# Windowed attention and a gated feed-forward block on one core: two heads in one double PSUM bank, feed-forward tiles of two blocks

## The chip, the cores and the metric

The kernel runs on one core of a Trainium2 chip. The metric is the device time of one execution in microseconds. The engines are TensorE (PE, matmuls), VectorE (DVE), ScalarE (ACT), GpSimd (POOL) and SyncE (SP, which issues most transfers). The tables of one core show all.

## The reference

Eight batches with eight heads each have 512 local and 32 global tokens of dimension 64. Local tokens see the global ones and the local ones within 32 positions; global tokens see all. The result, 4608 tokens of 512 features, goes through a feed-forward block with 2048 hidden units.

```python
s_ll = np.where(np.abs(pos[:, None] - pos[None, :]) <= 32, scale * q_l @ k_l.T, -1e9)
a_l = sm(np.concatenate([scale * q_l @ k_g.T, s_ll], axis=-1))
out_l = a_l @ np.concatenate([v_g, v_l])
out_g = sm(scale * q_g @ k_all.T) @ v_all
x = np.concatenate([out_g, out_l]).transpose(0, 2, 1, 3).reshape(4608, 512)
h = x @ w_in
sp = np.maximum(h, 0.0) + np.log1p(np.exp(-np.abs(h)))
out = (h * erf(sp)) @ w_out
```

## The kernel before

**The work.** Each float32 factor of the feed-forward block is split in two fp32r parts (names ending in h and l: xh, xl, winh, winl, wouth, woutl, gh, gl), and each product is three matmuls. The 4608 tokens are nine chunks: chunks 0 to 7 hold the 512 local tokens of a batch, chunk 8 the 256 global ones. The hidden units come in two halves, ps = 0 and ps = 1. For each chunk and half, `unit` (L1154) makes h for 256-row blocks in a PSUM bank and copies it to an SBUF tile hs; `gate` (L1180) runs softplus and erf on ScalarE (sp), multiplies by hs, rounds to gh and takes the rest gl; `project` (L1225) adds gh and gl times w_out into one PSUM bank per 128 tokens (op), which is evicted to os and stored. Half 0 leaves its sum in DRAM (part), half 1 adds it.

For half 1 of chunks 0 to 6, h is made by a scheme of seven products in place of eight: `seven_x` (L1055) forms sums of blocks of x (tx), `sums` (L1011) sums of weights (s0 to s3), and `quad` (L1103) runs seven products of 6 matmuls with 256 columns into four banks, two products in a bank, and adds them up on VectorE into two hs tiles. It does so for one column block of 128 hidden units at a time. Two of the four banks come from the pool ps_h (2 banks), two from ps_a (6 banks), which also serves attention and op.

The local attention (`attention`, L440) goes by windows of 32 rows on TensorE: scores of two heads into two banks s, a mask by matmul for the first heads (PREMASK of them) or on VectorE after that, maximum, exponential on ScalarE (sm). For the first TURN heads TensorE transposes the probabilities by matmul with the unit matrix ci; for the later ones VectorE does it in blocks of 32 (tp) and DMAs put the blocks in place (px, pt). `weighted` (L561) multiplies them by v (va, vb) into a bank o for each head, `weighted_end` (L589) divides by the sums into xn. `attention_global` (L694) does the global tokens of four heads in banks ga, gb and go, with GTURN in the role of TURN.

**The order.** All of these are entered with `Program.add` (L109) as operations with a planned duration per engine, a key and the tiles that they read and write. `Program.schedule` (L146) plays the engines through and emits the instructions in the order it finds: the ready operation with the least key, if its pool has a free tile. The numbers at the top of the file (HKEYS, QLEAD, WIN, LATE, AHEAD, SLACK and so on) set keys and limits. Where TensorE would idle before 53.6 us of the plan, it emits fillers, bf16 matmuls without use named spare. Waits between engines are semaphores that are put in for each tile. All engine calls go through helpers, so the profile's lines are those of the helpers: L348 (matmul), L349 (transpose), L350 (ScalarE), L351 (table load), L355 (DMA), L369 (VectorE and GpSimd). Names of tiles tell the place.

Of the kernel before, what the change touches and what calls it, by code (L numbers as in the profile page):

```python
# [20 lines left out]
P = 128  # L21
# [7 lines left out]
HKEYS = ((0, -7.804), (4, -5.172), (22, 1.403), (26, 7.192), (64, 43.381))  # L29
STEP, GKEY = 0.022, (-0.257, 0.006, -0.123)  # L30
QLEAD, VLEAD, RLEAD, XLEAD = (1.228, 0.782), (0.938, 0.499), 0.376, (1.072, 1.028, 1.005)
GOFF, POFF = (1.522, 1.5, 1.286), (4.244, 4.773, 2.878)
WIN, WOUT = (-5.905, -7.31, 0.441, -0.227), (10.721, 6.881, 8.147, 4.216)
LATE = (60.36, 53.234, 57.783, 66.337, 69.212, 67.928, 72.773, 74.4)
BIAS, AHEAD = 0.851, 10.286
# [12 lines left out]
BORROW = {"sm": ("sp", 7), "pt": ("hs", 7), "xn": ("gh", 5), "xT": ("gl", 5)}  # L48
# [3 lines left out]
BLOCK, ENTRY, FETCH = 256, 196, (5.06, 2.915)  # L52
START, RUSH, FETCHED = 2.5, 33.0, 1.0088
SWITCH, TRADE, CHOICE = 0.095, 0.092, 1

NBIAS, PREMASK = 5, 25
MLEAD = -5.339
# [3 lines left out]
PLAIN, MERGE = 0, 0  # L61
SEVEN = (0, 1, 2, 3, 4, 5, 6)
SUMS = (81.404, 83.062)

TURN, GTURN = 22, 6
GSPLIT = 4
# [18 lines left out]
class Buf:  # L85


    def __init__(self, pool, shape, dtype, name, tag, bufs=1):
        self.pool, self.shape, self.dtype, self.name, self.tag, self.bufs = pool, shape, dtype, name, tag, bufs
        self.users, self.ap = 0, None  # L90
        self.view = None
        self.writers, self.readers = [], []
# [6 lines left out]
class Program:  # L99
# [46 lines left out]
    def schedule(self):  # L146
# [74 lines left out]
        while events or any(o.eng is None for o in self.ops) and ahead < 1e3:  # L221
# [14 lines left out]
            while picked:  # L236
                picked = False
                for e, q in ready.items():
# [3 lines left out]
                    while until[e] <= now:  # L242
                        found = []
                        while q and len(found) < (CHOICE if e == "PE" else 1) and q[0][0] <= line[front].key + ahead:
# [4 lines left out]
                            need = {}  # L249
                            for b in op.new:  # L250
                                need[b.pool, b.tag] = need.get((b.pool, b.tag), 0) + 1
                            if any(free[k] < n for k, n in need.items()) or elsewhere(op, e):
# [42 lines left out]
                        for o in op.outs:  # L295
                            o.waits -= 1
                            o.at = max(o.at, t + (o.slack if e not in o.ways else 0.0))
# [12 lines left out]
def kernel(  # L310
# [29 lines left out]
    ps_a = ctx.enter_context(tc.tile_pool(name="ps_a", bufs=6, space=bass.MemoryType.PSUM))  # L340
# [53 lines left out]
    M16 = Buf(mp, [P, 512], F32, "mask16", "os", 2)  # L394
# [25 lines left out]
    def abuf(shape, name, tag, bufs):  # L420
# [4 lines left out]
        kind, n, h = name.split("_")[:3]  # L425
        if name == "vb_0_2":
# [3 lines left out]
        if kind in BORROW and int(n) * H + int(h) < FIRST:  # L430
            tag, bufs = BORROW[kind]
            b = Buf(mp, [P, SL], F32, name, tag, bufs)
            b.view = [P, 4, P]
# [3 lines left out]
    def psum_a(shape, name):  # L437
# [987 lines left out]
```

## Time and profile before

| | |
|---|---|
| median of 3 runs | 905.34 us (904.95 to 906.1) |
| profiled execution | 909.01 us, span 907.2 us |
| TensorE busy | 894.3 us (99%) |
| VectorE busy | 654.4 us (72%) |
| ScalarE busy | 521.7 us (58%) |
| GpSimd busy | 219.2 us (24%) |
| moved by DMA | 153.53 MB |

The time is that of the whole execution; the span is from the first to the last instruction in the trace. A busy share is a mean over stages. Matmuls overlap in the pipeline, so the distance from one start to the next, not the drawn length, is what one costs. A name such as h<-xh,winh reads: tile h written, from tiles xh and winh.

### The profile page before, as it was taken

How to read it: one execution, taken by the hardware profiler on the slowest of the kernel's cores; microseconds unless marked ns; L12 is line 12 of the kernel's file. 1: busy time of each engine (PE TensorE's matmuls, PEld its weight loads, DVE VectorE, ACT ScalarE, POOL GpSimd, SP SyncE). 2: the span in 40 equal slices, each digit the busy share in tenths (PEclk: the TensorE clock that was granted, in tenths of full speed). 3: DMA queues.
4: the chain of work that ended last, by engine and by line, in shares of the span. 5: the costliest groups of instructions: out<-in, count | busy, mean ns of one | idle time of the engine just before them, and what ended most of it. 6: DMA issues, size and time to landing. Idle time of an engine off the chain costs nothing.

```text
span 907.2 us, 22876 instructions
## 1 busy us (share of the span) xinstructions
PE 894.3 (99%) x9303; PEld 737.1 (81%) x9303; DVE 654.4 (72%) x1552; ACT 521.7 (58%) x949; POOL 219.2 (24%) x174
## 2 busy tenths in 40 slices
PE   9899999999999999999999999999999999999998
PEld 6676677777777777778898888989999999999896
DVE  4799886677576587685688759875868686868643
ACT  4668865635665457454666745565455554646452
POOL 0021314314544254110200202310323242321200
PEclk9999999999999999999999999999999999999999
DMA  9878979979979788985452400312325151321304
GB/s 345 337 264 292 276 220 278 314 223 250 333 239 304 238 233 303 253 280 144 169 163 94 150 12 1 70 47 47 102 39 133 26 121 48 93 76 41 94 1 116
DMA packets 93209, 153.53 MB, mean 169 GB/s; under 512 B 11952, under 2 KB 55728, under 8 KB 93104
## 3 DMA queue, kind: packets, MB, share of 16 engines
q1 hardware_dynamic: 92912, 151.81, 53.5%
q8 instruction: 73, 1.20, 0.6%
q10 hardware_dynamic: 192, 0.26, 0.1%
q14 instruction: 32, 0.26, 0.1%
HBM read 111.41 MB, written 40.63 MB: 168 GB/s over the span
## 4 chain that ended last, share of the span: by engine, by line
PE 85%; DVE 0%; SPq 0%; DMA 0%; ACT 0%; issue 0%; DVEq 0%
PE op L348 42%; PE h L348 36%; PE o L348 2%; PE s L348 2%; PE go L348 1%; PE ga L348 1%; SPq L355 0%; DMA px<-tp 0%; ACT os L350 0%; DVE sm L369 0%; DVE tp L369 0%; PE gb L348 0%; DVE os L369 0%; DVE mx L369 0%; DVE rs L369 0%
## 5 line engine op out<-in xcount | busy, mean ns | idle before, releaser
L348 PE MATMUL op<-wouth,gh 128*128 128x512 f32 x544 | 217.7, 400 | 0.3 <-DVE mx L369 0.3
L348 PE MATMUL op<-woutl,gh 128*128 128x512 f32 x544 | 212.7, 391 | 0.0
L348 PE MATMUL op<-wouth,gl 128*128 128x512 f32 x544 | 212.2, 390 | 0.0
L348 PE MATMUL h<-xh,winh 128*128 128x512 f32 (+1 forms) x464 | 165.1, 356 | 0.0
L348 PE MATMUL h<-xh,winl 128*128 128x512 f32 (+1 forms) x464 | 162.3, 350 | 0.0
L348 PE MATMUL h<-xl,winh 128*128 128x512 f32 (+1 forms) x464 | 162.1, 349 | 0.0
L369 POOL TENSOR_TENSOR sp<-sp,hs 128x512 f32<-128x512 f32 x51 | 73.1, 1450 | 309.5 <-ACT sp L350 249.2
L348 PEld LDWEIGHTS op<-wouth,gh 128*128 128x128 f32 x544 | 102.3, 188 | 26.5 <-issue 6.1
L348 PEld LDWEIGHTS op<-wouth,gl 128*128 128x128 f32 x544 | 102.2, 188 | 22.7 <-issue 0.4
L351 ACT ACT_TABLE_LOAD x90 | 115.5, 1283 | 2.3 <-PEq L1412 0.7
L348 PEld LDWEIGHTS op<-woutl,gh 128*128 128x128 f32 x544 | 102.5, 188 | 17.5
L350 ACT ACTIVATE gh<-sp 128x512 fp32r<-128x512 f32 x111 | 67.7, 629 | 81.1 <-DVE sp L369 57.4
L369 DVE TENSOR_TENSOR hs<-h,hs 128x256 f32<-128x256 f32 x196 | 77.3, 418 | 51.3 <-PE h L348 49.2
L348 PEld LDWEIGHTS h<-xh,winh 128*128 128x128 f32 x464 | 87.7, 189 | 16.3 <-issue 2.6
L350 ACT ACTIVATE sp<-hs 128x512 f32<-128x512 f32 x136 | 76.7, 622 | 36.8 <-DVE hs L369 36.4
L348 PEld LDWEIGHTS h<-xh,winl 128*128 128x128 f32 x464 | 87.7, 189 | 11.8
L348 PEld LDWEIGHTS h<-xl,winh 128*128 128x128 f32 x464 | 87.8, 189 | 11.7
L369 POOL TENSOR_TENSOR gl<-sp,gh 128x512 fp32r<-128x512 f32 x38 | 56.7, 1501 | 135.3 <-DVE gh L369 69.0
L350 ACT ACTIVATE hs<-h 128x512 f32<-128x512 f32 (+1 forms) x62 | 33.7, 543 | 93.5 <-PE h L348 93.3
L369 DVE TENSOR_TENSOR gl<-sp,gh 128x512 fp32r<-128x512 f32 x98 | 78.9, 827 | 5.3 <-ACT gh L350 4.1
L369 DVE TENSOR_TENSOR sp<-sp,hs 128x512 f32<-128x512 f32 x85 | 73.7, 894 | 4.6 <-ACT sp L350 4.6
L350 ACT ACTIVATE sp<-sp 128x512 f32<-128x512 f32 x136 | 74.9, 620 | 0.4
(179 smaller groups left out, 1483.5 us busy)
## 6 DMA issues: line engine op xcount, KB each, us to landing
vb<-in_vB_dram SPq DMA_DIRECT2D x32, 650.0 KB, 5.9
qk<-in_qk_dram SPq DMA_DIRECT2D x30, 656.0 KB, 6.9
rx<-xsc SPq DMA_DIRECT2D x52, 256.0 KB, 5.9
va<-in_vA_dram SPq DMA_DIRECT2D x32, 390.0 KB, 6.4
px<-tp SPq DMA_DIRECT2D x84, 128.0 KB, 4.2
pt<-px SPq DMA_DIRECT2D x21, 512.0 KB, 5.2
raw_in<-in_w_in_dram SPq DMA_DIRECT2D x16, 512.0 KB, 7.1
xsc<-xT SPq DMA_DIRECT2D x32, 256.0 KB, 5.5
```

Of the source, the lines that this page charges most:

```text
L348: pe = lambda n, *a, **k: pinned(nc.tensor.matmul(n, *a, **k))
L350: act = lambda *a, **k: pinned(nc.scalar.activation(*a, **k))
L351: table = lambda name: pinned(nc.scalar.preload_act_table_set(name))
L369: return lambda *a, **k: pinned(f(*a, **k))
```

## The change

The pool ps_a now has 3 tiles of two banks each (`banks`) in place of 6 single ones. A double bank has two marks (`half`) with which the planner tells its halves apart. Two heads are one operation chain: scores, values and the normalization of a pair share one tile s and one tile o; sm and mx hold both heads. ga and gb are the halves of one tile g. Two token blocks of op share a double bank.

In the feed-forward block hs, sp, gh and gl are tiles of 1024 columns, two blocks each (`pair`, 11 buffers for all four), and the operations of `gate` run over the whole. `quads` takes the place of `quad`: a product covers two column blocks (12 matmuls), the products with even number use the pool ps_h, the odd ones the halves of one double bank h_odd that stays in use to the end. Sums run on 512 columns, that of product 5 on 1024. The blocks of x are taken in place, without tx. Many numbers of the planner change, among them those below.

```diff
-HKEYS = ((0, -7.804), (4, -5.172), (22, 1.403), (26, 7.192), (64, 43.381))
+HKEYS = ((0, -31.7886), (4, -21.8895), (22, 5.2526), (26, 6.0605), (64, 49.4687))
-WIN, WOUT = (-5.905, -7.31, 0.441, -0.227), (10.721, 6.881, 8.147, 4.216)
+WIN, WOUT = (-28.7173, -46.2072, 7.6294, -4.7711), (26.2493, 21.6004, -11.9103, 42.1867)
-NBIAS, PREMASK = 5, 25
+NBIAS, PREMASK = 20, 21
-TURN, GTURN = 22, 6
-GSPLIT = 4
+TURN, GTURN = 19, 4
+SMS = 2
+GSPLIT = 3
...
-    ps_a = ctx.enter_context(tc.tile_pool(name="ps_a", bufs=6, space=bass.MemoryType.PSUM))
+    ps_a = ctx.enter_context(tc.tile_pool(name="ps_a", bufs=3, space=bass.MemoryType.PSUM))
...
+    pair = lambda name, dtype=F32, spare=0: Buf(mp, [P, 2 * SL], dtype, name, "pair", PAIRS, spare)
+    def banks(name):
+
+        b = Buf(ps_a, [P, 2, 512], F32, name, "a", 3)
+        b.half = [mark(), mark()]
+        return b
...
+        for i in range(2):
+            new = [O] if O is not S and i == 0 else []
+            add({"PE": 0.64}, key + STEP * (3 + i), lambda i=i: values(i), [PT, VA, VB, *([] if new else [O])], [*new, O.half[i]], heat=1040, fetch=64, mode=1)
...
+            if k % 2 == 0:
+                bank = Buf(ps_h, [P, 2, half], F32, f"h_{name}_{k}", "h", 2)
+                at, reads, new = lambda: bank.ap, [bank], [bank]
+            else:
+                if not odd:
+                    odd.append(banks("h_odd"))
+                r, bank = k // 2 % 2, odd[0].half[k // 2 % 2]
+                at, reads = lambda: odd[0].ap[:, r].rearrange("p (q x) -> p q x", q=2), [odd[0], bank]
+                new = [bank] if odd[0] in prog.allocated else reads
...
+        at, reads = product(0, "11", "11")
+        add({"ACT": 0.2 + 0.0007 * n, "DVE": 0.15 + 0.00095 * n}, key, lambda e: copy(e, part(0, L), at()), [*reads, *H], [own[0, 0]])
+        plus(1, product(1, "s2", "t2"), 1, L, 0, L)
+        plus(2, product(2, "12", "21"), 0, L, 0, L)
+        plus(3, product(3, "s1", "t1"), 1, R, 1, L)
+        plus(4, product(4, "s4", "22"), 0, R, 1, R)
+        at5, reads5 = product(5, "s3", "t3")
...
-            add({"DVE": 0.62, "POOL": 1.35}, k, lambda e, SPb=SPb, Hb=Hb: vec[e].tensor_tensor(SPb.ap, SPb.ap, Hb.ap, ALU.mult), [Hb], [SPb])
+            add({"DVE": 1.22, "POOL": 2.5},
+                k,
+                lambda e, SPb=SPb, Hb=Hb: vec[e].tensor_tensor(mine(SPb.ap), mine(SPb.ap), theirs(Hb.ap), ALU.mult),
+                [Hb, *marks],
+                [SPb],
+            )
...
-            OP = [psum_a([P, DM], f"op_{ps}_{c}_{t}") for t in range(nt)]
+            OB = [banks(f"op_{ps}_{c}_{t}") for t in range(0, nt, 2)]
+            OP = [(OB[t // 2], t % 2) for t in range(nt)]
```

**TensorE in the seven products.** The first piece is from half 1 of chunk 3, before, where one bank of products (h_1_3_0_0) is full and the next (h_1_3_0_1) begins; the second is the same chunk after, where product 2 ends and product 3 begins in the double bank.

```order
L348 MATMUL h_1_3_0_0_9515<-xh_1_3_1_9405,s1h_7939 128x256
L348 MATMUL h_1_3_0_0_9515<-xl_1_3_1_9424,s1h_7939 128x256
L348 MATMUL h_1_3_0_0_9515<-xh_1_3_1_9405,s1l_7948 128x256
L348 MATMUL h_1_3_0_1_9528<-xh_1_3_1_9405,winh_1_0_7064 128x256
L348 MATMUL h_1_3_0_1_9528<-xl_1_3_1_9424,winh_1_0_7064 128x256
L348 MATMUL h_1_3_0_1_9528<-xh_1_3_1_9405,winl_1_0_7065 128x256
```

```order
L352 MATMUL h_1_3_0_2_8600<-xh_1_3_1_8467,winh_1_0_7108 128x256
L352 MATMUL h_1_3_0_2_8600<-xl_1_3_1_8471,winh_1_0_7108 128x256
L352 MATMUL h_1_3_0_2_8600<-xh_1_3_1_8467,winl_1_0_7109 128x256
L352 MATMUL h_odd_7457<-xh_1_3_0_8449,s0h_6998 128x256 [waits DVE_49]
L352 MATMUL h_odd_7457<-xl_1_3_0_8452,s0h_6998 128x256
L352 MATMUL h_odd_7457<-xh_1_3_0_8449,s0l_7073 128x256
```

A row that waits for an engine's semaphore ends with its name. Before, the next bank starts without a wait. After, the first matmul of product 3 waits for VectorE (DVE_49), whose count stands for the eviction of product 1 from the other half of h_odd; the first of product 5 has the same wait for product 3.

**VectorE beside it.** The additions of chunk 3's first column block before, and of its first pair of column blocks after (the rows on h_odd are products 1, 3 and 5), with the gate operations of chunk 2 (sp, gl) between them.

```order
L369 COPY hs_1_3_0_9541<-h_1_3_0_0_9515 128x256 [waits PE_49]
L369 TENSOR_TENSOR hs_1_3_4_9543<-h_1_3_0_0_9515,hs_1_3_0_9541 128x256 [waits DVE_49]
L369 TENSOR_TENSOR hs_1_3_0_9541<-h_1_3_0_1_9528,hs_1_3_0_9541 128x256 [waits DVE_49,PE_49]
L369 TENSOR_TENSOR hs_1_3_4_9543<-h_1_3_0_1_9528,hs_1_3_4_9543 128x256
L369 TENSOR_TENSOR sp_1_2_2_9470<-sp_1_2_2_9470,hs_1_2_2_9266 128x512 [waits Activation_49]
L369 TENSOR_TENSOR hs_1_3_0_9541<-h_1_3_0_2_9494,hs_1_3_4_9543 128x256 [waits DVE_49]
L369 TENSOR_TENSOR hs_1_3_4_9543<-h_1_3_0_2_9494,hs_1_3_4_9543 128x256 [waits DVE_49]
```

```order
L373 TENSOR_TENSOR hs_1_3_0_1_8570<-h_odd_7457,hs_1_3_0_0_8569 128x2x256 [waits PE_49,Activation_49]
L373 TENSOR_TENSOR gl_1_2_2_0_8616<-sp_1_2_2_0_8527,gh_1_2_2_0_8598 128x1024 [waits Activation_49]
L373 TENSOR_TENSOR hs_1_3_0_0_8569<-h_1_3_0_2_8600,hs_1_3_0_0_8569 128x2x256 [waits DVE_49,PE_49]
L373 TENSOR_TENSOR gl_1_2_2_1_8644<-sp_1_2_2_1_8528,gh_1_2_2_1_8614 128x1024 [waits Activation_49]
L373 TENSOR_TENSOR hs_1_3_0_1_8570<-h_odd_7457,hs_1_3_0_1_8570 128x2x256 [waits PE_49]
L373 TENSOR_TENSOR hs_1_3_0_0_8569<-h_1_3_0_4_8631,hs_1_3_0_1_8570 128x2x256 [waits DVE_49,PE_49]
L373 TENSOR_TENSOR hs_1_3_0_1_8570<-h_odd_7457,hs_1_3_0_1_8570 128x1024 [waits DVE_49,PE_49]
L373 TENSOR_TENSOR hs_1_3_0_1_8570<-h_1_3_0_6_8660,hs_1_3_0_1_8570 128x2x256 [waits DVE_49,PE_49]
```

Before, additions have 256 columns and gate operations 512; after, additions have 512 (one 1024) and a gate operation of 1024 columns stands between product 1 and product 2, and between product 2 and product 3.

**TensorE in the values of two heads.** Batch 5, heads 0 and 1: the end of the first head's products with v and what follows, before; the end of both heads' products after, which start 20 rows earlier in one piece (o_5_0).

```order
L348 MATMUL o_5_0_4478<-va_5_0_3912,pt_5_1_4370 32x65
L348 MATMUL op_0_2_0_4015<-wouth_0_2_1376,gh_0_2_4_4173 128x512
L348 MATMUL op_0_2_0_4015<-woutl_0_2_1377,gh_0_2_4_4173 128x512
L348 MATMUL op_0_2_0_4015<-wouth_0_2_1376,gl_0_2_4_4179 128x512 [waits Pool_49]
L348 MATMUL op_0_2_0_4015<-wouth_0_2_1376,gh_0_2_5_4294 128x512 [waits Activation_49]
L348 MATMUL op_0_2_0_4015<-woutl_0_2_1377,gh_0_2_5_4294 128x512
L348 MATMUL op_0_2_0_4015<-wouth_0_2_1376,gl_0_2_5_4304 128x512 [waits Pool_49]
L348 MATMUL o_5_1_4514<-va_5_0_3912,pt_5_1_4370 32x65 [waits DVE_49]
L348 MATMUL o_5_1_4514<-vb_5_0_4038,pt_5_1_4370 32x65 x2
```

```order
L352 MATMUL o_5_0_4258<-vb_5_0_3910,pt_5_0_4122 32x65 x2
L352 MATMUL o_5_0_4258<-va_5_0_3786,pt_5_0_4122 32x65
L352 MATMUL h_0_3_6_4302<-xh_0_3_0_3590,winh_0_3_505 128x512
L352 MATMUL h_0_3_6_4302<-xl_0_3_0_3605,winh_0_3_505 128x512
L352 MATMUL h_0_3_6_4302<-xh_0_3_0_3590,winl_0_3_506 128x512
```

Before, six matmuls of the projection (op) stand between the two heads, and the second waits for VectorE; after, the two heads run through, and the dense matmuls of h follow.

## Rows read from the trace of the kernel before

**Rows 1.** The page: busy time, bytes moved in 40 slices, chain by engine.

```profile
PE 894.3 (99%) x9303; PEld 737.1 (81%) x9303; DVE 654.4 (72%) x1552; ACT 521.7 (58%) x949; POOL 219.2 (24%) x174
...
GB/s 345 337 264 292 276 220 278 314 223 250 333 239 304 238 233 303 253 280 144 169 163 94 150 12 1 70 47 47 102 39 133 26 121 48 93 76 41 94 1 116
...
PE 85%; DVE 0%; SPq 0%; DMA 0%; ACT 0%; issue 0%; DVEq 0%
```

**Rows 2.** Windows: span, then busy us of each engine (its name first), clock, DMA.

```profile
25.00:50.00 25.00, 22.51 (x563) 16.35 (x546) 20.01 (x46) 15.01 (x41) 2.41 (x1) 0.93 0.83 315
50.00:100.00 50.00, 48.23 (x916) 36.43 (x900) 48.87 (x107) 36.16 (x95) 10.22 (x7) 1.00 0.82 264
350.00:850.00 500.00, 500.00 (x3519) 434.21 (x3518) 367.58 (x737) 285.05 (x457) 107.00 (x85) 1.00 0.35 104
850.00:907.20 57.20, 52.92 (x301) 46.30 (x299) 26.09 (x47) 26.93 (x37) 6.04 (x5) 1.00 0.30 83
```

**Rows 3.** Waits of TensorE: group, releaser, us in total, times, longest.

```profile
PE ga L348 <- issue: 2.5, 1, 2.5
```

**Rows 4.** Timeline of TensorE: start us, length us, operation, tiles, shape, count.

```profile
171.00 0.39 PE L348 MATMUL h<-xh,winl 128*128 128x512 f32 x1
171.32 0.24 PE L348 MATMUL o<-va,pt 128*32 128x65 f32 x1
...
172.20 0.23 PE L348 MATMUL o<-vb,pt 128*32 128x65 f32 x2
172.22 0.22 PE L348 MATMUL o<-va,pt 128*32 128x65 f32 x1
172.37 0.50 PE L348 MATMUL op<-wouth,gh 128*128 128x512 f32 x1
172.71 0.40 PE L348 MATMUL op<-woutl,gh 128*128 128x512 f32 x1
172.95 0.40 PE L348 MATMUL op<-wouth,gl 128*128 128x512 f32 x1
```

**Rows 5.** Timeline of TensorE at 701 us.

```profile
701.05 0.28 PE L348 MATMUL h<-xl,s0h 128*128 128x256 f32 x1
701.17 0.28 PE L348 MATMUL h<-xh,s0l 128*128 128x256 f32 x1
```

**Rows 6.** Timeline of TensorE at 51 and 53 us: fillers (spare) and transposes.

```profile
50.87 0.72 PE L348 MATMUL spare<-const-bfloat16-1.0 128*128 128x256 bf16 x5
51.52 0.61 PE L348 MATMUL ga<-qk 64*32 64x480 f32 x4
...
53.49 1.09 PE L349 MATMUL s<-ci,sm 128*128 128x128 f32 x8
54.34 0.48 PE L348 MATMUL h<-xh,winh 128*128 128x512 f32 x1
```

**Rows 7.** Timeline of SyncE at 3.6 us: DMA issues.

```profile
3.56 2.13 SPq L355 DMA_DIRECT2D raw_in<-in_w_in_dram  x2
```

**Rows 8.** Timeline of VectorE at 696 to 702 us.

```profile
695.77 1.29 DVE L369 TENSOR_TENSOR xl<-tx,xh 128x512 fp32r<-128x512 f32 x2
...
701.50 0.75 DVE L369 TENSOR_TENSOR hs<-h,hs 128x256 f32<-128x256 f32 x2 [0.56 <-PE h L348]
702.17 1.48 DVE L369 TENSOR_TENSOR sp<-sp,hs 128x512 f32<-128x512 f32 x1
```

**Rows 9.** Groups of VectorE and GpSimd: count, busy us, mean ns, idle before.

```profile
L369 DVE TENSOR_TENSOR gl<-sp,gh 128x512 fp32r<-128x512 f32 x98 | 78.9, 827 | 5.3 <-ACT gh L350 4.1
...
L369 DVE TENSOR_TENSOR sp<-sp,hs 128x512 f32<-128x512 f32 x85 | 73.7, 894 | 4.6 <-ACT sp L350 4.6
...
L369 DVE TENSOR_TENSOR winl<-raw_in,winh 128x1024 fp32r<-128x1024 f32 x7 | 8.6, 1233 | 0.0
...
L369 POOL TENSOR_TENSOR sp<-sp,hs 128x512 f32<-128x512 f32 x51 | 73.1, 1450 | 309.5 <-ACT sp L350 249.2 <-PE h L348 34.4 <-DVE hs L369 14.4
```

**Rows 10.** Timeline of VectorE at the end.

```profile
902.96 0.69 DVE L369 TENSOR_TENSOR os<-op,pr 128x512 f32<-128x512 f32 x1 [0.67 <-PE op L348]
```

More of the change, by code (lines that the diff above doesn't have):

```diff
@@ L620, in wide @@
+        add({"DVE": 0.61, "ACT": 1.74}, key + STEP * 3, norm, [O, *O.half, RS], [XN])
+        XT = abuf([P, 4, P], f"xT_{nm}", "xT", 1)
+        if b == 0:
+            straight(p, XN, XT, O, nm, key + STEP * 4)
+        else:
+            turned(b, p, XN, XT, key + STEP * 4)
+        if p % 2 == 1:
+            attention_global(b, p // 2, key + GKEY[min(b, 2)])
     def wide(view, name, tag):
@@ L712, in scores @@
                 for f in range(2):
-                    for r, T in enumerate((GA, GB)):
+                    for r in range(2):
                         c0 = WB * (2 * i + f)
@@ L1152, in quad, with part @@
-        return list(zip(H, S))
+        n = SL if c < B else B * SG
+        half = n // 2
+        name = f"{ps}_{c}_{q}"
+        L, R = slice(0, half), slice(half, n)
+        H = [pair(f"hs_{name}_{i}", F32, SPARE[0]) for i in range(2 if c < B else 1)]
+        own = {(i, z.start): mark() for i in range(2) for z in (L, R)}
+        def part(i, z):
+            t = H[i if c < B else 0].ap.rearrange("p (q x) -> p q x", q=2)
+            z0 = z.start + (0 if c < B else n * i)
+            return t[:, :, z0 : z0 + z.stop - z.start]
@@ new lines, in plus @@
+        def plus(k, bank, i, z, j, y):
+            at, reads = bank
+            add({"DVE": 0.15 + 0.00105 * n},
+                key + QUAD * k,
+                lambda: dve.tensor_tensor(part(i, z), at(), part(j, y), ALU.add),
+                [*reads, *H, own[j, y.start]],
+                [own[i, z.start]],
+            )
+        at, reads = product(0, "11", "11")
+        add({"ACT": 0.2 + 0.0007 * n, "DVE": 0.15 + 0.00095 * n}, key, lambda e: copy(e, part(0, L), at()), [*reads, *H], [own[0, 0]])
@@ new lines, in quads @@
+        plus(1, product(1, "s2", "t2"), 1, L, 0, L)
[3 more added lines that the diff above has]
+        at5, reads5 = product(5, "s3", "t3")
+        both = lambda: part(1, slice(0, n)).rearrange("p q (h x) -> p q h x", h=2)
+        add({"DVE": 0.15 + 0.00105 * 2 * n},
+            key + QUAD * 5,
+            lambda: dve.tensor_tensor(both(), at5().unsqueeze(2).to_broadcast([P, 2, 2, half]), both(), ALU.add),
+            [*reads5, *H],
+            [own[1, 0], own[1, half]],
+        )
@@ L1154, in unit @@
+        plus(6, product(6, "22", "t4"), 1, L, 1, L)
+        us = []
+        for i in range(2 if c < B else 1):
+            marks = [own[i, 0], own[i, half]] if c < B else [*own.values()]
+            us.append((H[i], pair(f"sp_{name}_{i}", F32, SPARE[1]), marks))
+        return us
     def unit(ps, c, v, X, key):
```

662 lines of the change are left out of this document (317 added, 345 removed).

## The prediction

> **What bounds the kernel now.** I read the page first. TensorE is busy 894.3 of 907.2 us, and the chain that ended last is TensorE's for 85% [rows 1]. So I looked for the 12.9 us in which it is not busy: by windows it loses 2.5 us in 25 to 50 us, 1.8 in 50 to 100, nothing at all from 350 to 850 us, and 4.3 in the tail after 850 [rows 2], which leaves 8.6 us before 350, at a granted clock of 1.00 (the 2.4 GHz level) but for 0.93 in 25 to 50. The list of waits names only small ones, the longest 2.5 us on nothing that the profile shows [rows 3]. In the full part a change in another engine's work is worth nothing unless it makes TensorE wait; what counts is what TensorE itself executes, and which semaphores it must pass.
>
> **The price of a TensorE row.** A matmul's drawn length (0.39 us) overlaps the next, so I price by start to start. A 512-column feed-forward matmul costs 0.23 to 0.24 us (172.71 to 172.95) and a 256-column one 0.12 (701.05 to 701.17) [rows 4, 5]. The change from dense 128x128 work to the 32-row attention products and back is visible at 171 us: the last dense matmul before them takes 0.32 to the next start (0.09 over 0.23), the last small one 0.15 (0.13 over the 0.02 from its neighbour), and the first dense one after them 0.34 (0.11 over) [rows 4]. A round trip costs 0.33 us. A 128-column transpose is (54.34 - 53.49)/8 = 0.106 us, a filler of 256 columns (51.52 - 50.87)/5 less the 0.09 of the mode change = 0.112 [rows 6]; a mask matmul has 512 columns, 0.23.
>
> **The change part by part.**
>
> *A, TensorE work that goes.* The 1392 + 1632 main feed-forward matmuls stay, column for column, apart from their order. By the order of both kernels the attention of two heads now runs through without dense work between the heads more often: 74 entries into small-tile work in place of 89, so 15 round trips x 0.33 = 5.0 us. More pairs go through the DMA transposition (TURN 22 to 19, GTURN 6 to 4): 88 to 80 transposes of probabilities and 36 to 24 of global ones, 20 x 0.106 = 2.1 us. Masks by matmul fall from 26 to 22: 4 x 0.23 = 0.9. Together -8.0 us. In the full stretches this is a gain without a condition; in the stretches with idle time (the first 350 us) it is a gain only if TensorE isn't waiting there anyway. The bounds are -8.0 and, if half of the switches only turn into waiting, about -4.
>
> *B, the start.* SyncE's order puts the first input-weight load (two transfers of 512 KB) ahead of the mask and the first q/k, where it was seventh [rows 7]. At the 345 GB/s of the page's first slice [rows 1], 1.05 MB are 3.0 us by which the first scores come later. The order shows what the planner lays into that hole: 37 fillers in place of 25 before the first scores, and 136 in place of 121 over the whole start, 13 more of 256 columns and 2 more of 512: 13 x 0.112 + 2 x 0.23 = +1.9 us. The first feed-forward matmul stands at the same progress of the attention in both. Fillers stand where the planner expects waiting, so this prices the wait as the planner sees it. Bound above: the full 3.0 us and half again as much idle time as the 8.6 us now before 350, +7.3. Bound below: VectorE, at 98% in 50 to 100 us [rows 2], is relieved, half of the 8.6 us goes, and so does the clock's dip (7% of 25 us), -6. I take +1.9, the nearest to what the order shows.
>
> *C, the double bank of the odd products.* Now each of seven products for a column pair is 12 matmuls of 256 columns, 12 x 0.12 = 1.43 us. Even ones use two single banks in turn, odd ones the two halves of one double bank, and a semaphore stands for the whole tile: product 3 waits for the eviction of product 1 although it writes the other half, and product 5 for that of 3. That is 2 waits x 14 column pairs = 28, each with only one product, 1.43 us, in front of it. Before, a bank came round after four banks' work. The eviction starts 0.33 us after the last matmul's start (701.17 to 701.50) [rows 5, 8] and takes about 0.65 to 0.69 on 512 columns (the two 256-column ones there 0.75 together; a 512-column add with another source 1.29/2) [rows 8]. With VectorE idle, and 0.1 (my guess) for the way back, that is 0.33 + 0.67 + 0.1 = 1.1, against the 1.43 + 0.12 = 1.55 until the next odd product: no stall. But VectorE also runs gate operations, now 1024 columns in one piece, 1.23 us by the nearest row (winl) [rows 9]. In VectorE's order after (the section on the change shows it), a 1024-column gl stands between the evictions of 1 and 2, and one between 2 and 3. With the last matmul's start of product 1 at 0: eviction 0.33 to 1.0, gl to 2.23, eviction of 2 (ready at 1.76) to 2.9, gl to 4.13, eviction of 3 to 4.8, and product 5, which could start at 3 x 1.43 + 0.12 = 4.41, starts at 4.9, 0.5 late. This pattern stands in 4 chunks: 2.0 us. In the second column pairs GpSimd runs beside VectorE in about six places, where a 512-column product takes up to 1.48 in place of about 0.65 [rows 8], and I add 0.1 for each: C = +2.6 us. Bounds: 0 (VectorE always in time), and, with a gate operation of 1.23 just begun before every one of the 28 evictions, 1.1 + 1.23 - 1.55 = 0.78 each, 22.
>
> The Trainium skill ("Perfetto Trace Analysis", Matmuls) says that independent groups should rotate through different PSUM banks, so that the evacuation of one runs beside the matmuls of the next. This kernel's rotation is by tile, so that rule speaks against the double bank; by it the 28 waits would all count, and C would be the upper bound. The trace of before, which rotates four banks, has no such wait from 350 to 850 us [rows 2], which agrees with the rule but doesn't price its breach.
>
> *D, wider vector work.* VectorE's rows fall from 1430 to 1101, ScalarE's from 808 to 590, GpSimd's from 154 to 76 (sp products on GpSimd 51 to 7, gl 38 to 2). In time it's near nothing for VectorE: 85 + 98 gate operations of 512 become 61 + 66 of 1024, 127 x 1.23 = 156 us against 73.7 + 78.9 = 152.6 now [rows 9]. What goes is GpSimd's 1.45 us operations [rows 9] and their contention. While TensorE is full none of it shows, so 0, with the small gain in the bound of B.
>
> The Trainium skill ("Perfetto Trace Analysis", Optimizing Scalar/DVE Operations) gives about 60 ns of overhead for each VectorE instruction; 329 fewer would then be an estimate of 20 us of VectorE time. The same section says that smaller pieces can be done sooner where they hold up another engine. The rows show 1.29 for two 512-column operations against 1.23 for one of 1024, 0.06 saved, which agrees with the first; TensorE's full windows say that it is the second sentence that could decide here, by C.
>
> *E, the tail.* Both halves of the last output tile now share one double bank, and the order makes the first eviction wait for the last matmul of both. Now the two tiles are evicted apart, and one eviction (902.96, 0.69 long) lies behind the last matmul [rows 10]. After, both do: one more of 0.69, bounds 0 and 1.4. I take +0.7.
>
> *Sum.* -8.0 + 1.9 + 2.6 + 0 + 0.7 = -2.8 us. The profiled execution is 909.0 us (span 907.2 and 1.8 around it), 3.7 above the median of 905.34 of the runs shown; set off from that median, the forecast is **902.5 us**. The forecast's own range, with C between 0 and 6 and B between -1 and +4, one at a time, is about 899.5 to 906.
>
> **The rivals.**
> 1. *The double bank decides (slower).* The rows of the order on TensorE show the wait, and VectorE's gate operations of 1.23 us can stand ahead of any of the 28 evictions. Against it: one product covers an undisturbed eviction, and VectorE is idle for a quarter of 350 to 850 us [rows 2]. With the 0.5 of the pattern above at each of the 28 the time is 902.5 - 2.6 + 14 = 913.9; the kernel is slower than before from a mean stall of (8.0 - 1.9 - 0.7)/28 = 0.19 us upward.
> 2. *The start gets longer (slower).* Two heads in one tile mean that nothing of the first starts before both are scored; with the late first scores the bound of B gives 902.5 - 1.9 + 7.3 = 907.9. For it: VectorE at 98% there; against: the planner's order keeps the same progress at the first feed-forward matmul.
> 3. *The savings fall where TensorE waits (no change).* Half of A goes, and B and C stay: 902.5 + 4 = 906.5. For it: the switches that go lie in the attention, the part with idle time. Against it: the idle time is 8.6 us in 350.
> 4. *Contention goes (faster).* With GpSimd nearly out of the gates, VectorE's 894 ns sp products come down to half of 1.23 us [rows 9], evictions come in time, C is 0 and the start loses 3 us of idle time: 902.5 - 2.6 - 3 = 896.9.
>
> **How the numbers follow.** Chances: the forecast 0.40, the first rival 0.17, the second 0.13, the third 0.15, the fourth 0.15. A measurement of this kernel can tell about 0.2%, 1.8 us, from no change: faster is below 903.5, slower above 907.2. Faster: half of the forecast's cases and a bit (0.27), all of the fourth (0.15) and some of the third (0.03): 0.45. Same: 0.12 of the forecast, 0.08 of the third, 0.03 of the first two: 0.23. Slower: the rest, 0.32. The range for 8 in 10 leaves out the fourth's far end and the first's upper half: 895 to 914 us.
>
> **What would show it.** A: TensorE's small-tile groups in the profile after have the same counts but fewer changes, and 20 fewer transposes. B: first scores about 3 us later, and the first h matmul 1 to 3 us later than 54.34. C: on the list of TensorE's waits, "h_odd" behind VectorE's hs, some 4 to 10 times with 0.3 to 0.8 us, between 350 and 850 us, where there is no wait now; 28 of them would be the first rival. E: two os operations after the last matmul. I am wrong if TensorE's busy time (the start-to-start sum in full stretches) doesn't fall by some 6 to 8 us, if h_odd's waits come to more than 8 us, or if idle time before 350 us changes by more than 5 us.

## The result and the profile after

The changed kernel takes 915.16 us (median of 6 runs, 913.62 to 917.28), the kernel before in the same comparison 906.14 us (6 runs, 904.95 to 907.79): ratio 1.0098, 95% interval 1.0082 to 1.0115. It is 1% slower, where 0.3% faster was forecast, and just outside the range. The profiled executions are 917.28 and 909.01 us.

The page after (lines as in [rows 1]):

```profile
PE 891.6 (97%) x9294; PEld 738.8 (81%) x9294; DVE 613.5 (67%) x1169; ACT 507.8 (55%) x710; POOL 145.4 (16%) x86
...
PE 85%; DMA 5%; DVE 4%; ACT 3%; issue 1%; SPq 1%; DVEq 0%
```

TensorE is busy 2.7 us less, VectorE 41, GpSimd 74 us less; yet the span grows from 907.2 to 915.5. So TensorE's idle time grows by 8.3 + 2.7 = 11.0 us, from 12.9 to 23.9. The windows after (columns as in [rows 2]) say where:

```profile
0.00:110.00 110.00, 100.16 (x2025) 73.13 (x2026) 87.09 (x143) 65.25 (x166) 11.97 (x11) 1.00 0.86 295
...
350.00:850.00 500.00, 499.64 (x3731) 432.88 (x3716) 341.92 (x505) 291.71 (x344) 76.88 (x47) 1.00 0.41 118
...
850.00:915.50 65.50, 60.17 (x350) 53.13 (x349) 25.99 (x33) 20.75 (x23) 0.00 (x0) 0.98 0.25 73
...
110.00:350.00 240.00, 231.62 (x3199) 179.71 (x3205) 158.46 (x491) 130.04 (x179) 56.56 (x30) 0.98 0.79 250
```

The two long ones for the kernel before, of the same view:

```profile
0.00:110.00 110.00, 103.64 (x2099) 75.32 (x2102) 90.02 (x198) 73.89 (x191) 16.18 (x16) 0.98 0.86 302
110.00:350.00 240.00, 237.75 (x3406) 181.23 (x3389) 170.73 (x573) 135.86 (x266) 89.93 (x69) 1.00 0.85 266
```

Idle before 110 us: 9.8 in place of 6.4. From 110 to 350 us: 8.4 in place of 2.3. From 350 to 850, 0.4 in place of none; in the tail 5.3 in place of 4.3. The list of TensorE's waits names the largest single one:

```profile
PE s L352 <- issue: 4.5, 3, 2.4
PE op L352 <- ACT pg L354: 3.6, 1, 3.6
PE s L353 <- issue: 3.2, 2, 1.6
PE s L353 <- ACT sm L354: 1.6, 3, 0.8
```

An output matmul doesn't read pg, a tile of the global attention. What joins them is a bank. TensorE and ScalarE there:

```profile
233.50 0.39 PE L352 MATMUL op<-woutl,gh 128*128 128x512 f32 x1
233.72 0.39 PE L352 MATMUL op<-wouth,gl 128*128 128x512 f32 x1
237.73 0.80 PE L352 MATMUL op<-wouth,gh 128*128 128x512 f32 x1 [3.62 <-ACT pg L354]
238.33 0.63 PE L352 MATMUL op<-woutl,gh 128*128 128x512 f32 x1
238.75 0.63 PE L352 MATMUL op<-wouth,gl 128*128 128x512 f32 x1
```

```profile
227.93 0.60 ACT L354 ACTIVATE hs<-h 128x512 f32<-128x512 f32 x1 [1.37 <-PE h L352]
228.55 1.28 ACT L355 ACT_TABLE_LOAD   x1
229.84 2.01 ACT L354 ACTIVATE sp<-hs 128x1024 f32<-128x1024 f32 x2
231.87 1.28 ACT L355 ACT_TABLE_LOAD   x1
233.17 2.00 ACT L354 ACTIVATE sp<-sp 128x1024 f32<-128x1024 f32 x2
235.19 1.28 ACT L355 ACT_TABLE_LOAD   x1
236.48 1.20 ACT L354 ACTIVATE pg<-g,gn 128x96 f32<-128x96 f32 x4
```

The new op tile got the double bank of the global scores g, whose last reader, pg, stands on ScalarE behind a whole gate of 1024-column pieces with its three table loads, 228.55 to 236.47. TensorE stands still from 233.95 to 237.73. After it the matmuls follow at 0.43 us (238.33 to 238.75) in place of 0.23, which is the 1.2 GHz level (the granted clock of 237.7 to 244 us is 0.51); 14 of them, about 2.8 us more. Another of the three double banks, that of s of the pair before, was free from about 234.1 us, when VectorE ends its last maximum. The planner had counted with the bank that is free first; the pool that hands out the tiles goes round in its own order. The run on banks below tests this reading.

### The profile page after: what moved, and what is told of

Its sections match the earlier page's. It is cut to its first block, busy times and chain, and to the rows that moved or that the text cites. A ratio compares the mean times of both kernels' runs of the same rounds, so it can differ in the third digit from the quotient of the medians.

```text
span 915.5 us, 21963 instructions
## 1 busy us (share of the span) xinstructions
PE 891.6 (97%) x9294; PEld 738.8 (81%) x9294; DVE 613.5 (67%) x1169; ACT 507.8 (55%) x710; POOL 145.4 (16%) x86
## 4 chain that ended last, share of the span: by engine, by line
PE 85%; DMA 5%; DVE 4%; ACT 3%; issue 1%; SPq 1%; DVEq 0%
PE op L352 38%; PE h L352 30%; PE h_odd L352 7%; PE s L352 4%; PE o L352 2%; DMA px<-tp 2%; PE g L352 1%; DMA rx<-xsc 1%; PE go L352 1%; PE s L353 1%; ACT sp L354 1%; DVE raw_in L373 1%; SPq L359 1%; PE spare L352 1%; DMA raw_out<-in_w_out_dram 1%
## 5 line engine op out<-in xcount | busy, mean ns | idle before, releaser
L354 ACT ACTIVATE hs<-h 128x512 f32<-128x512 f32 x75 | 44.9, 600 | 135.5 <-PE h L352 135.3
L373 DVE TENSOR_TENSOR sp<-sp,hs 128x1024 f32<-128x1024 f32 x61 | 78.2, 1314 | 54.9 <-ACT sp L354 54.9
L354 ACT ACTIVATE sp<-hs 128x1024 f32<-128x1024 f32 x68 | 69.3, 1054 | 39.0 <-DVE hs L373 38.5
L373 DVE TENSOR_TENSOR gl<-sp,gh 128x1024 fp32r<-128x1024 f32 x66 | 81.7, 1248 | 10.1 <-ACT gh L354 9.8
L354 ACT ACTIVATE gh<-sp 128x1024 fp32r<-128x1024 f32 x63 | 65.9, 1060 | 25.3 <-DVE sp L373 18.2
L354 ACT ACTIVATE sp<-sp 128x1024 f32<-128x1024 f32 x68 | 68.4, 1052 | 0.4
L373 POOL TENSOR_TENSOR xl<-rx,xh 128x512 fp32r<-128x512 f32 (+1 forms) x25 | 35.9, 1448 | 165.2 <-ACT xh L354 91.6
L373 POOL TENSOR_TENSOR rx<-rx 128x512 f32<-128x512 f32 x21 | 31.3, 1489 | 187.8 <-DVE xl L373 183.8
L373 POOL TENSOR_TENSOR sm<-sm,mx 128x1024 f32<-128x1024 f32 x17 | 34.3, 2020 | 156.4 <-DVE mx L373 138.5
```

What stands on the lines that cost most here:

```text
L354: act = lambda *a, **k: pinned(nc.scalar.activation(*a, **k))
L373: return lambda *a, **k: pinned(f(*a, **k))
```

## The experiments

Unless said otherwise a time is the median, and the ratio is to the kernel before in the same comparison.

**Numbers or structure.** Many of the planner's numbers changed with the structure; two were set back, then all; and the kernel before got the new ones of the fetch.

```diff
 after, first run:
-FETCH = (1.6245, 1.9095); START = -20.0182
+FETCH = (5.06, 2.915); START = 2.5
 after, second run: HKEYS to SUMS, WIN, WOUT, TURN, GTURN, PREMASK as before; QUAD = 0.3
 before, third run:
-FETCH = (5.06, 2.915); START = 2.5
+FETCH = (1.6245, 1.9095); START = -20.0182
```

> The changed kernel with two of the planner's numbers set back (the assumed time for TensorE's instruction fetch, and the assumed start of the transfers). Theory N (the planner's new numbers): three stalls of 1.8 us in the middle of a run of scores or transposes, where no semaphore is open, are instruction fetch that the new numbers leave out of the plan; with the old numbers they go, and the time falls by 3 to 5 us to 910 to 912. Theory S (structure: two heads in one double bank, which is released as a whole): the stalls behind PSUM stay, the time stays at 914 to 916.

> The changed kernel's structure with all of the planner's numbers that both kernels have as they were before (keys, leads, fetch, masks, turns). Theory N: most of the 9 us goes, 904 to 908. Theory S: the waits for double banks and for both heads stay, and the numbers don't suit the new structure, 913 to 925. The first weight load is no longer ahead of the first q and k.

> The kernel before with the planner's two new numbers of fetch and start of transfers. Theory N: stalls inside runs of matmuls appear where there was one of 2.6 us, the time rises by 3 to 5 us to 909 to 911. Theory S: within 1.5 us of before, 905 to 907.5.

Measured: 918.05 us (1.0141, 1.0122 to 1.0160), 934.93 us (1.0338, 1.0308 to 1.0368) and 908.1 us (1.0027, 1.0007 to 1.0047). Neither set of old numbers helps the new structure; the new ones cost the old structure 0.3%, between what the two theories gave. With all old numbers the largest wait is

```profile
PE s L352 <- issue: 12.0, 6, 4.0
```

So setting the numbers back doesn't take the loss away. But each of these kernels is a new plan, and the two that follow show what that can cost; numbers against structure stays undecided by these three.

**One load, and TURN.** In the changed kernel the first weight load went back behind the first q/k; in the kernel before, fewer heads are masked and turned on TensorE (TURN is 20, for with heads in pairs the changed kernel's 19 turns 20).

```diff
 after:
-WIN[1] = -46.2072
+WIN[1] = -31.5
 before:
-PREMASK = 25; TURN, GTURN = 22, 6
+PREMASK = 21; TURN, GTURN = 20, 4
```

> The changed kernel with the key of the first input-weight load moved so that it is issued behind the first masks, q, k and v as before. If the start costs what my step B says, the first scores come 3 us sooner and the time falls by 1.5 to 3 us, to 912 to 913.5. If the start has slack up to the first feed-forward matmul, the time stays within 1 us.

> The kernel before with the numbers of masks and turns of the changed one alone (PREMASK 21, TURN 20, GTURN 4). If step A's prices hold where TensorE is busy, 20 transposes and 4 masks less are worth 3 us: 902 to 903.5. If pairs that go through the DMA transposition cost waits at the start, no gain or a loss: 905 to 909.

Measured: 935.51 us (1.0337, 1.0297 to 1.0377) and 917.27 us (1.0145, 1.0116 to 1.0175). Both lie 8 us or more above all that was expected, the second in a kernel whose TensorE work only fell. In the first, the start did come sooner: first scores at 6.96 us and first h at 50.99 us, 2.0 and 5.1 us ahead of the changed kernel. What it loses lies behind, with 17.6 us idle from 110 to 350 us. There it has these longest waits:

```profile
PE s L352 <- issue: 6.1, 2, 4.3
PE op L352 <- POOL woutl L373: 2.9, 1, 2.9
PE s L352 <- ACT pg L354: 2.3, 1, 2.3
```

Any number changed lets the planner order thousands of operations anew. These five new plans lost 3 to 21 us, and I put that down to the new order rather than to the numbers; no run shows it. Such a run can't carry a verdict on one part; from here on the order stays as it is, word for word, but for the run on pairs and a few entries moved by hand below.

**Which bank.** The plan's own bank for each tile, in the same order of work: the planner keeps a list of free slots, first freed first out, and the tile is put there.

```diff
+                            slots[b.pool, b.tag].append(b.slot)   # when a tile is freed
...
+                        for b in op.new:
+                            b.slot = slots[b.pool, b.tag].pop(0)  # when it is planned
...
+            if b.pool is ps_a:
+                b.tag, b.bufs = f"a{b.slot}", 1
```

> The changed kernel with the same plan, word for word; only the choice of the double bank is made by the plan (the one that came free first in it) and not by the tile pool, which gave the tile op_0_2_2 the double bank that g_4_1 still held until ScalarE's exponentials behind 8 us of softplus and erf, while that of s_4_3 was free 3.6 us sooner. Theory P (the wait at 233.7 us is the choice of the bank): the wait of 3.8 us shrinks to below 0.5, the clock's dip behind it goes too, and the time falls by 4 to 6 us, to 909 to 911. Theory Q (three double banks are too few whichever is taken): another wait takes its place, the time stays within 1.5 us of 915.

> The kernel before with the choice of the bank made by the plan, as a control for the same edit on six single banks. With six banks the choice should matter little: within 2 us of 905. If it gains 2 us or more, the edit's gain on the changed kernel is not a matter of double banks.

Measured: the changed kernel comes down to 909.2 us (908.1 to 911.74; 1.0051, 1.0033 to 1.0070), the kernel before moves little, to 904.03 us (0.9978, 0.9959 to 0.9997). The wait for pg is gone, and 110 to 350 us has 3.6 us idle in place of 8.4:

```profile
0.00:110.00 110.00, 98.01 (x2003) 72.47 (x2019) 86.21 (x142) 64.05 (x165) 11.13 (x10) 0.98 0.84 290
110.00:350.00 240.00, 236.41 (x3307) 184.51 (x3306) 166.74 (x517) 139.45 (x187) 58.74 (x31) 1.00 0.83 265
```

Against the kernel before in the same comparison the loss falls from 9.0 to 4.5 us (1.0098 to 1.0051): about 4.5 us, half of it, are the choice of the bank. With six single banks the same edit gains 0.2%, 0.7 us by the medians, so it is mostly a matter of three double banks, though the intervals don't shut out a common part. Three more profiles check this and the start: of the changed kernel as it is, and of both kernels with the plan's banks.

> A second profile of the changed kernel as it is. Theory B (banks): the wait of op for ACT's pg at 233.7 us (3.8 us) is in the order of the program, so it stands in this execution too, 3 us or longer; the first h may come anywhere from 52 to 58 us. Rival V: that wait was an event of one execution; here it is under 1 us.

> A second profile of the changed kernel with the plan's own banks (909.2 us; first h at 57.0 us). Theory V: the start of this kernel differs by several us from execution to execution (52.3 and 57.6 us in two of one kernel), because instruction fetches fall beside different waits; the first h comes more than 1 us away from 57.0 us. Theory F: the start is fixed by the two-head chain; the first h comes at 56 to 58 us.

> The same for the kernel before with its plan's own banks (904.0 us; first h at 53.8 us; the kernel before 54.3 us). Theory V and F: first h at 53 to 55 us, since six single banks hold more heads side by side and one late head is covered; rival: its start scatters as widely as that of the changed kernel, and then no difference of the two starts is shown.

The wait stands in the changed kernel's second execution (911.17 us) at the same matmul, now with no fall of the clock behind it (next start after 0.33, then 0.23):

```profile
230.50 0.39 PE L352 MATMUL op<-wouth,gl 128*128 128x512 f32 x1
234.48 0.50 PE L352 MATMUL op<-wouth,gh 128*128 128x512 f32 x1 [3.59 <-ACT pg L354]
234.81 0.39 PE L352 MATMUL op<-woutl,gh 128*128 128x512 f32 x1
235.04 0.39 PE L352 MATMUL op<-wouth,gl 128*128 128x512 f32 x1
```

In the one with the plan's banks (913.01 us) it doesn't. Its first h came at 56.3 us, as theory F had it; that of the kernel before with the plan's banks (902.64 us) at 52.0, sooner than the theories V and F said. The windows of these two, first the changed kernel's:

```profile
0.00:110.00 110.00, 98.73 (x1943) 71.71 (x1944) 83.42 (x139) 60.59 (x155) 9.97 (x9) 0.95 0.82 280
110.00:350.00 240.00, 236.54 (x3365) 183.91 (x3363) 165.96 (x518) 139.36 (x194) 60.00 (x31) 1.00 0.83 263
```

```profile
0.00:110.00 110.00, 104.77 (x2140) 75.83 (x2141) 91.39 (x204) 77.49 (x202) 19.07 (x17) 1.00 0.91 315
110.00:350.00 240.00, 239.66 (x3435) 184.25 (x3434) 169.41 (x584) 138.83 (x263) 89.05 (x70) 1.00 0.87 270
```

Before 110 us TensorE is idle 6.4, 5.3 and 5.2 us in the three profiles of the old structure, and 9.8, 9.8, 12.0 and 11.3 us in the four of the new one. In all nineteen traces, over several plans, it is 4.7 to 7.4 us with the old structure (seven traces) and 8.5 to 12.8 with the new one (twelve). So more idle time in the start goes with the structure. A late first h doesn't: the changed kernel with its first load put back has 11.3 us idle and its first h at 50.99 us, and a single execution scatters by some us.

**Banks by twos in the kernel before.** Single banks stay, but two are taken and given back together.

```diff
+    twins.append((GA, GB))                  # also both s, both o, go with a spare bank, op by twos
+    # a tile keeps its bank until its twin's last user is done; both are taken at once
```

> The kernel before, whose six banks are now taken and given back two at a time (two scores, two values, ga and gb, two tiles of the projection, and a second bank for each go): the supply of the changed kernel without its wider operations. Theory Q: this alone costs 4 to 10 us, 909 to 915. Theory R (the numbers and the longer operations cost it, not the supply): 904 to 908.

Measured: 920.41 us (1.0171, 1.0149 to 1.0193). It is a new plan, so the 16 us aren't a price. One thing in it counts: the start does not suffer, and the stretch behind it does.

```profile
0.00:110.00 110.00, 105.26 (x2136) 76.51 (x2144) 91.42 (x205) 77.63 (x202) 19.31 (x17) 1.00 0.90 315
110.00:350.00 240.00, 235.22 (x3219) 178.50 (x3218) 161.90 (x521) 134.78 (x258) 66.22 (x50) 0.99 0.79 250
```

With 4.7 us idle before 110 us, banks by twos alone need not make the start longer.

**What holds the start.** All on the plan's banks (909.2 us) and its order. First 19 entries of the list were moved (the expectation says 23): the conversions of two weight blocks on VectorE, which stood ahead of the first maxima, go behind them; then the first load and one maximum as well.

```diff
-    for op in prog.schedule():
+    plan = list(prog.schedule())    # raw_in_0_1: behind pt_0_0 and xn_0_0; raw_in_0_0: behind xl and pt_0_2
...
+    plan = [plan[i] for i in sorted(range(len(plan)), key=lambda i: place.get(i, i))]
+    for op in plan:
```

> The changed kernel with the plan's own banks (909.2 us), its list of work unchanged but for 23 entries: the two weight blocks raw_in_0_1 and raw_in_0_0 are turned to floats on VectorE behind the maxima, the pt copy and the divided sums of the first pairs instead of ahead of them (they stood at 6.4 to 11.1 us ahead of mx, and at 18.6 to 23.3 us ahead of xn). Theory W: the rest of the loss sits in the start because two-head chains queue behind these blocks; mx begins about 1.9 us sooner, the 1.7 us wait for xn at 22.4 us goes, the first h starts 2 to 3.5 us before 57.0 us and the kernel takes 905.5 to 907.5 us. Rival F: what holds the start is the length of the two-head chain itself (maximum, eight exponentials, transposes, copy) and the stretches in which TensorE waits for nothing in the records (1.9, 2.6 us); then the first h moves by under 1 us and the time stays at 908.5 to 910 us. Rival D: the freed VectorE time is taken back at 35 to 50 us, where the blocks now stand; the first h comes no sooner, and the time is 909 to 911 us.

> As the run beside it, and two more entries of the list moved: the load of raw_in_0_1 behind the loads of mask, qk, va and vb of the first two heads (it stood ahead of all of them, and the first scores waited 0.4 us for qk), and the second half of the maxima of s_2_3 ahead of the xl subtractions (s_3_0 waited 1.6 us for them at 113 us). Theory W: first scores about 0.9 us sooner (8.1 us), the wait at 113 us down to about 0.4 us, together 1.5 to 2.2 us below the run beside it: 903.5 to 905.5 us, level with the kernel before (904.7 us). Rival F: these waits are replaced by others further on, since the next chain ends no sooner; within 0.7 us of the run beside it.

Measured: 915.47 us (1.0103, 1.0076 to 1.0130) and 915.42 us (1.0104, 1.0080 to 1.0129), 5 us worse in place of better. In the first of them the maximum does begin sooner, at 10.17 us in place of 11.03, and the time is taken back where the blocks now stand (first h at 58.1 us in place of 57.0, the hundredth 512-column h or op matmul at 110.1 in place of 110.0). And something new comes at 348 us, far from every entry that moved:

```profile
PE op L356 <- DVE mx L377: 2.2, 1, 2.2
```

```profile
345.51 0.71 DVE L377 STREAM_TRANSPOSE tp<-sm 128x512 f32<-128x512 f32 x1 [2.13 <-DMA px<-tp]
```

A tp tile was still being read by a DMA; VectorE waited 2.13 us for it, the maximum behind it came later, the double bank that it frees came later, and TensorE stood for 2.2 us. So moving the weight conversions behind doesn't shorten the start, and with three double banks one late transfer reaches TensorE. It isn't the whole of the 5 us: the second run has no such stop and is as slow, with its first h at 62.03 us.

Then the chain itself: one exponential per head in place of four in the first heads (it subtracts the maximum of the head's first 128 columns from all 512), the same in the kernel before; a second profile; and a maximum over those 128 columns only.

```diff
-            for j in range(4 * i, 4 * i + 4):
-                act(SM.ap[:, j, :], src()[:, j, :], AF.Exp, bias=MX.ap[:, j : j + 1], scale=f)
+            j = slice(4 * i, 4 * i + 4)
+            act(SM.ap[:, j, :], src()[:, j, :], AF.Exp, bias=MX.ap[:, 4 * i : 4 * i + 1], scale=f)
```

> The changed kernel with the plan's own banks (909.2 us), same list of work; in the masked-first heads each head's four exponentials are one instruction on 128x512, which takes the maximum of its first 128 columns for all four (the softmax is the same, only what is subtracted before the exponential differs). Theory F: at the start TensorE waits because a pass now carries two heads through one chain: eight exponentials of 0.38 us stand between its scores and its first transposes; the four waits for sm (2.4 us together, none in the kernel before) go, the first h starts 1.5 to 3 us before 57.0 us, and the time is 905.5 to 907.5 us. Rival I: these waits only stand ahead of the ones on instruction fetch (1.9, 2.6 us) and on xn, which come later but as long; the time stays at 908.5 to 910.5 us.

> The same edit in the kernel before with its plan's own banks (904.0 us): one exponential for the four of a head. Control. Theory F: no wait of TensorE for sm stands in its trace, since six heads stand side by side in single banks, so shorter exponentials release nothing: 903 to 905 us. If it gains as much as the run beside it, the gain there is of shorter exponentials in general and says nothing of the two-head pass.

> One more look at the changed kernel with the plan's own banks and one exponential per head: its profiled execution took 904.4 us and its other eight 907.2 to 912.3 us. Theory F: the start is the same in every execution (first h at 52 to 53 us, hundredth 512-column matmul at about 105 us), and what differs between executions comes behind it. Rival I: the early start was luck of that execution; in one of 907 us or more the first h comes at 55 us or later.

> As the changed kernel with the plan's own banks and one exponential per head, and in those heads the maximum too is taken over the first 128 columns of each head alone, the 128x256 that the exponential uses (1.21 us on 1024 columns before; estimated 0.4 us): the chain from scores to transposes is 0.8 us shorter in each pass of the start. Theory F: another 0.5 to 2 us less than the run with one exponential (909.3 us median): 907 to 909 us, and the first h at 50 to 52 us. Rival I: the time of the whole no longer answers to the start, since the waits on double banks behind it take what the start gives: 908.5 to 910.5 us, though the first h comes sooner.

Measured: 909.3 us (904.37 to 912.32; 1.0049, 1.0023 to 1.0074); the control 904.24 us (0.9995, 0.9978 to 1.0012); the second profile 911.25 us; the shorter maximum 908.78 us (906.45 to 912.06; 1.0041, 1.0024 to 1.0058). The windows before 110 us of the profiled run, of the second profile and of the shorter maximum:

```profile
0.00:110.00 110.00, 101.16 (x2140) 75.40 (x2155) 92.31 (x165) 59.45 (x104) 13.81 (x12) 1.00 0.89 307
```

```profile
0.00:110.00 110.00, 100.39 (x2016) 73.32 (x2017) 85.74 (x142) 54.53 (x99) 10.77 (x10) 0.98 0.85 290
```

```profile
0.00:110.00 110.00, 101.50 (x2090) 74.74 (x2090) 81.61 (x160) 58.33 (x103) 13.01 (x11) 1.00 0.87 305
```

Idle falls to 8.8, 9.6 and 8.5 us, from 12.0 and 11.3 (9.8 twice without the plan's banks), and the waits for sm from 1.5 to 3.1 us to at most 1.2. So 1 to 2 us of the start are the wait for two heads' exponentials; but the control's trace has 7.4 us idle, 2 more than its two traces without the edit, so that is also what executions scatter by. The medians don't follow (909.3 and 908.8 against 909.2; 908.78 lies in the ranges of both theories), and the two executions of one kernel have their first h at 52.32 and 57.55 us, as the rival had it. The second one lost its time to waits of this kind, at 53 us:

```profile
PE g L356 <- issue: 3.5, 2, 2.9
```

Theory F is right about the wait for sm, and not shown as the cause of the remaining 4 us of the whole.

## Why the prediction was wrong

**A, TensorE's own work: right, somewhat smaller.** The 20 transposes are gone (124 to 104 in the traces). Start to start over the whole trace, without fillers and without idle time of over 0.25 us, the matmuls take 872.0 us in the second profile of the kernel before with the plan's banks and 866.5 in that of the changed kernel as it is, the two without a fall of the clock ahead of the last matmul: -5.5 us, where -8.0 was forecast. In the two first profiles, with the matmuls at 1.2 GHz counted at half, it is 873.6 and 866.6: -7.0. The gain is there, and is spent elsewhere.

**B, the start: right in sign, wrong in kind.** The first load does go ahead, but the first scores come 1.0 us later, not 3.0 (8.97 against 7.99); the first h comes at 56.06 us, 1.7 later, inside the 1 to 3. What failed is the price: I took the planner's fillers for the wait. There are 136 of them in place of 121, but start to start they come to 20.7 us, against 20.6, so that term is nothing; the wait stands beside them as idle time, which grew by 3.5 us before 110 us, against +1.9. Waits for sm are in it that the kernel before didn't have (1.6 us in the list above; 0.9 us in one later trace of the old structure).

**C, the double bank: this is the step that failed, in its place.** The forecast looked for the double bank's price in h_odd, where it was easy to work out, and there it is almost nothing. The tile's own view, why VectorE sat idle before its evictions, and who waited for them:

```profile
L373 DVE TENSOR_TENSOR hs<-h_odd,hs x42: 681/692/1225, 580.5 to 863.2; 128x512 f32<-128x512 f32 x28, 128x1024 f32<-128x1024 f32 x14
its engine sat idle before it (us, times) until:
  PE h_odd L352: 24.6, 18
...
who waited for it (us, times):
...
  PEld h_odd L352: 0.8, 4
```

0.8 us in four waits of TensorE's weight loads, not 2.6 and far from the 22 of the bound: it was mostly VectorE that waited for h_odd (24.6 us). The four are where the prediction put them, at product 5 of the first column pair in four chunks (711, 753, 795 and 838 us), but the matmul starts 0.28 us after the one before it in place of 0.12: 0.16 late, not 0.5. The pattern was right, its size was not.

The same change in the three double banks of ps_a for s, o, g and op had no term at all in the sum, and no rival had late banks there (the second has two heads in one tile, but as a chain at the start). There a tile keeps two banks until the last reader of either half is done, and only three are to be had. That made TensorE's stop from 233.95 to 237.73 us with 2.8 us of slower matmuls behind it. A stop of 2.4 us at 111 us, with 1.7 us of slower matmuls behind it, is of the same kind:

```profile
114.03 1.87 PE L352 MATMUL s<-qk 64*32 64x128 f32 x64 [2.42 <-issue]
```

The profile names no releaser. But these scores start 0.1 us after VectorE's last maximum of an earlier pair's s, which stood behind 3.63 us of xh<-rx and two subtractions xl; and in the second run on the start, which put those maxima ahead of the subtractions, the scores start 0.1 us after the last maximum again (116.09 us), with no stop. The idle time from 110 to 350 us grew by 6.1 us. The first rival named the right mechanism in the wrong stretch; its time, 913.9, comes near for another reason.

The Trainium skill ("Perfetto Trace Analysis", Matmuls) says that independent groups should rotate through different PSUM banks. Its rule is borne out here not where I applied it: in h_odd a rotation over two halves of one tile costs 0.8 us, since 1.43 us of matmuls lie between; in op a rotation over three double banks cost about 4.5 us, since a bank there is held by other engines' work.

**D, wider vector work: right for the gates.** Their sp and gl on VectorE take 159.9 us, about as forecast (156). VectorE as a whole is 41 us less busy, most of it in the additions and copies of hs (110.4 to 78.3 us, lengths added up), and none of it shows in the full part. (The 60 ns that the prediction took from the Trainium skill, "Perfetto Trace Analysis", Optimizing Scalar/DVE Operations, are that page's figure for operands in SBUF; for PSUM, which the additions of hs read, it gives about 125 ns, so the estimate of 20 us doesn't hold for all 329 instructions.) One consequence was missed: the gate's 1024-column operations make one block of 228.55 to 236.47 us on ScalarE, and pg, which frees a bank, stands behind it.

**E, the tail: right.** Both halves are evicted behind the last matmul (1.29 us in place of 0.69), and the tail's idle time grows by 1.0:

```profile
910.21 1.29 DVE L373 TENSOR_TENSOR os<-op,pr 128x512 f32<-128x512 f32 x2 [7.06 <-PE op L352]
```

**The sum by what was measured.** For the two first profiles: work -7.0 us (A); matmuls at the lower clock +4.2 (4.8 us in the changed kernel's, 0.6 in the other); fillers +0.1; idle +3.5 before 110 us, +6.1 to 350, +0.4 to 850, +1.0 in the tail: +8.3, which is the span's growth. Of my three conditions for being wrong, the third came true: idle time before 350 us grew by 9.6 us.

**What stays open.** The choice of the bank accounts for about 4.5 of the 9 us. The rest, 4 to 5 us against the kernel before, is what remains when the smaller work is set against more idle time, with the plan's banks 6.3 us more before 110 us, 2.5 from 110 to 350 and 1.1 in the tail (two traces of each). The idle time in the start goes with the structure, with all the old numbers too (11.6 us); that the two-head pass makes it isn't shown. Neither is what it is worth in the whole, for the order of the work changed with the structure and stands as a rival that no run separates: the changed kernel with its load put back begins h sooner than either kernel, and is slower. Shorter exponentials take back some of the idle time but no time that the medians show. The waits on issue aren't needed for the idle time: the kernel with its load put back has none over 0.9 us before 110 us, and 11.3 us idle there. No run beats the kernel before by more than its 0.2%: the best is that kernel with the plan's own banks, 904.03 us.

## What to carry to other kernels

When tiles are merged, list for every pool the number of pieces that circulate and the last reader of each, on all engines; a buffer that is released by the slowest of two readers behind a long block on its engine is a wait of the next tile, whatever that tile computes. Where a planner counts free buffers, make the tile pool hand out the very buffer that it counted. Test a part of a planned kernel with the order frozen, for a new plan moves the time by more than the part.

## What the runs showed of the hardware

A stop in the middle of a run of small matmuls, with nothing to wait for, stands in most profiles of the start. In the changed kernel's, TensorE stops after 45 of 64 score matmuls:

```profile
27.94 0.91 PE L352 MATMUL s<-k,q 64*32 64x128 f32 x45
30.52 0.62 PE L352 MATMUL s<-k,q 64*32 64x128 f32 x19 [1.68 <-issue]
```

One packet of the queue for instructions moves just then; the DMA view of 27.9 to 29.1 us:

```profile
q1 hardware_dynamic: 134, 0.49, 101.4%
q8 instruction: 1, 0.02, 5.6%
```

It is 16 KB and lies from 27.97 to 29.04 us, and TensorE goes on 1.5 us after its end; at 36 and 73 us it is the same (1.3 and 1.5 us), and for fillers at 22 us (1.5 us). The eleven others that end before 110 us have no such stop behind them. In the kernel before the longest is 2.5 us [rows 3]. That a stretch of small instructions can run ahead of its own fetch while the loads fill the DMA engines is what these rows suggest; no run tried it by itself. It may be why two executions of one kernel start up to 5 us apart.
